# Attention and a gated layer on one core: GpSimd casts the higher part of a weight piece in the first four turns

## The chip, the cores and the metric

The kernel runs on one core of a Trainium2 chip. A core has five engines with an instruction queue each, which run in order and wait for one another by semaphores: TensorE (PE; its weight loads are listed as PEld), VectorE (DVE), ScalarE (ACT), GpSimd (POOL) and SyncE (SP), which issues most DMAs. The metric is the time of one execution on the device in microseconds (us), as a median of runs.

## The reference

Causal block attention for 8 batches of 8 heads, 576 tokens of 64 numbers each, then a gated layer on the 4608 tokens of 512 numbers:

```python
scores = scale * np.matmul(q, k.transpose(0, 1, 3, 2))
scores = np.where(block_i >= block_j, scores, -1000000000.0)   # blocks of 64 positions
attn = np.exp(scores - np.max(scores, axis=-1, keepdims=True))
attn = attn / (np.sum(attn, axis=-1, keepdims=True) + 1e-09)
x = np.matmul(attn, v)            # then [B, H, S, D] -> [B * S, H * D]
h = x @ w_in                      # w_in: 512 x 2048
out = (h * (1.0 / (1.0 + np.exp(-1.702 * h)))) @ w_out   # w_out: 2048 x 512
```

Everything comes in fp32. The weights w_in and w_out are stored as 64-bit numbers.

## The kernel before

**Turns.** Two heads make a pair, and there are 32 pairs. The main loop makes one turn per pair (turn 0 to turn 32). A turn does the scores of its pair (five row chunks 0 to 4, of widths 64, 192, 320, 448 and 576), the values (the product with v) of the pair before, and the transposition of q and k for the pair to come. The strings ORDER, START and HANDOVER give the order in a turn: digits are score chunks, L is `prep` (the two DVE transpositions of L297 that make `qk` for the next pair), V is `av`, and a, B, C are `flip` (PE transposes finished weights of attention, L102, and ACT copies them out of PSUM, L411 and L424; a takes chunks 0 and 1, B takes 2 and 3, C takes 4).

**One chunk** passes PE (scores, L99), DVE (a pass that masks, scales and finds the row's minimum, L351), ACT (exp with the row sum, L358), DVE (two tiny steps on the sums `sm`, L368 and L371), POOL (scaling by 1/sum, L376), then PE, ACT and PE again for B, C or a and V. V ends in two ACT copies into `xr` (L451, L450). DVE, ACT and POOL run in order, so an instruction that waits holds up all that stands behind it.

**Weight pieces.** There are 32 pieces of 128x512, in groups of four for w_in and four for w_out. A piece is converted in three steps. `begin` (L219): ACT takes the upper words into a PSUM bank of its own (tag w3, one buffer). `merge` (L223, L229, L234): DVE puts an fp32 number together in three instructions and writes it to a tile `wm` (two buffers in turn). `split_weights` (L243 and L82): a copy rounds that number to fp32r, the higher part (`wih` or `woh`), and POOL subtracts it to get the lower part (`wil` or `wol`). `begin` of the next piece follows `split_weights` in program order, and needs the bank that `merge` reads. `convert` spreads the pieces over turns by WEIGHTS_BY: by the end of turn 3 in program order 12 pieces are through, and by turn 8 all 32. On the engines they run later than in program order: the casts of those 12 pieces run from 20 us to 93 us. The tile scheduler puts each engine's instructions in an order by its own estimates of costs and by priorities, so PE's list and the lists of the other engines need not follow the text.

**The gated layer** (`moe`) is a generator from which `advance` takes work in step with the turns. It takes 384 tokens at a time (12 tiles, TILES). `split` makes a higher part `xh` (ACT, L498) and a lower part `xl` (DVE subtract, at L82) of the tokens. For each of 16 slices PE makes `hp` in 12 products (three for each of four parts of w_in), ACT and DVE make the gate `g` (L562, L563), ACT and POOL split it into `gh` and `gl` (L571, L82), and PE adds the slice to `acc`. `hp` has one PSUM bank, so the next slice waits until L563 has read the last one. The layer begins when the first batch's four pairs have their values, that is after V of turn 4.

The change touches `split_weights` alone; its line L243 is the cast on ACT, and the counter `turns["n"]` is the turn in program order (HP is 4).

Of the kernel before, what the change touches and what calls it, by code (L numbers as in the profile page):

```python
# [40 lines left out]
def attention_moe_kernel(  # L41
# [9 lines left out]
    nc = tc.nc  # L51
# [12 lines left out]
    HP = H // 2  # L64
# [6 lines left out]
    def f(ap):  # L71
        return ap.bitcast(F32)
# [8 lines left out]
    def subtract(eng, out, in0, in1):  # L81
        eng.tensor_tensor(out=out, in0=in0, in1=in1, op=ALU.subtract)  # L82
# [3 lines left out]
    turns = {"n": 0, "bank": 0, "experts": False}  # L86
# [37 lines left out]
    def weights(name, g):  # L124
        if (name, g) not in home:
            home[name, g] = room(f"{name}{g}", [P, 4, WC], F32R, name)
        return home[name, g]
# [111 lines left out]
    def split_weights(j):  # L239
        _, name, g, x = pieces[j]  # L240
        z = whole.pop(j)
        hi, lo = (weights(name + p, g)[:, x] for p in "hl")
        nc.scalar.copy(out=hi, in_=f(z))  # L243
        subtract(nc.gpsimd, lo, f(z), f(hi))

    def convert(upto):

        while conv["step"] < int(2 * upto):
            j, odd = divmod(conv["step"], 2)
            if odd:  # L250
                split_weights(j)
                if j + 1 < len(pieces):
                    load_weights(j + 3)
                    begin(j + 1)
            else:
                if j == 0:
                    begin(0)
                merge(j)
            conv["step"] += 1
# [405 lines left out]
```

## Time and profile before

| | us |
|---|---|
| median of 3 runs | 1117.67 (1117.2 to 1118.97) |
| span of the profiled execution, first to last instruction | 1116.9 |
| PE busy | 1082.2 (97% of the span) |
| DVE, ACT, POOL busy | 584.2, 498.9, 406.4 |
| PE busy from 200 us to the end | 909.5 of 917 |

The profiled execution is known by its span only, 1116.9 us; the median of the runs is 0.8 us longer, which lies around the span. PE is busy nearly all the time after the first fifth, so the table says little about what waits for what in the first 90 us, where the changed instructions run. For that stretch the trace is read in order of time, and the waits are read in windows.

### The profile page before, as it was taken

To read this page: it belongs to the slowest core of one execution; us is meant where nothing else is said; L and a number is where in the kernel's file an instruction comes from. 1 tells how busy PE (TensorE), PEld (TensorE's weight loads), DVE (VectorE), ACT (ScalarE), POOL (GpSimd) and SP (SyncE) were. 2 spreads that over 40 slices of the span, in tenths; PEclk is the share of its full clock that TensorE was granted. 3 is DMA by queue.
4 is the path that set the end of the run, shared out by engine and by line. 5 is a ranking of instruction groups with operands and counts; after the bars stand their busy time and mean duration, and the time that the engine had idled before them with its cause. 6 is when DMAs were issued, how large, how long until landed. Compare 5 with 4: busy or idle time off the path is not lost. (4 is left out here: it accounts for less than half of the span.)

```text
span 1116.9 us, 19972 instructions
## 1 busy us (share of the span) xinstructions
PE 1082.2 (97%) x6960; PEld 912.9 (82%) x6960; DVE 584.2 (52%) x1856; ACT 498.9 (45%) x1321; POOL 406.4 (36%) x509
## 2 busy tenths in 40 slices
PE   6979999999999999999999999999999999999998
PEld 4757777788888888888888888888888888899997
DVE  6786786655645645655555555645645654211210
ACT  5865775443533534534443443443444434322322
POOL 4665565332333333333333332333333333122222
PEclk8979999999999999999999999999999999999999
DMA  8634523342434433243443333344442332200000
GB/s 183 193 89 153 146 61 80 72 103 59 96 81 86 109 80 70 58 99 71 113 86 75 80 92 68 63 108 86 86 103 66 71 84 54 54 30 1 29 1 29
DMA packets 219365, 91.25 MB, mean 82 GB/s; under 512 B 197760, under 2 KB 197760, under 8 KB 219264
## 3 DMA queue, kind: packets, MB, share of 16 engines
q1 hardware_dynamic: 214528, 89.38, 34.1%
q8 instruction: 55, 0.90, 0.3%
q10 hardware_dynamic: 4736, 0.59, 0.3%
q14 instruction: 46, 0.38, 0.1%
HBM read 45.09 MB, written 9.44 MB: 49 GB/s over the span
## 5 line engine op out<-in xcount | busy, mean ns | idle before, releaser
L82 POOL TENSOR_TENSOR gl<-g,gh 128x384 fp32r<-128x384 f32 x192 | 194.5, 1013 | 555.1 <-ACT gh L571 450.4
L563 DVE SCALAR_TENSOR_TENSOR g<-g,hp 128x384 f32<-128x384 f32 x192 | 106.0, 552 | 318.6 <-ACT g L562 317.2
L99 PE MATMUL hp<-xh,wih 128*128 128x384 f32 x768 | 265.8, 346 | 2.8 <-DVE g L563 1.8
L562 ACT ACTIVATE g<-hp 128x384 f32<-128x384 f32 x192 | 94.2, 491 | 368.5 <-PE hp L99 361.0
L99 PE MATMUL hp<-xh,wil 128*128 128x384 f32 x768 | 258.7, 337 | 0.0
L99 PE MATMUL hp<-xl,wih 128*128 128x384 f32 x768 | 254.4, 338 | 0.2
L99 PE MATMUL acc<-woh,gh 128*128 128x512 f32 x576 | 233.9, 406 | 0.0
L99 PE MATMUL acc<-wol,gh 128*128 128x512 f32 x576 | 227.0, 394 | 0.0
L99 PEld LDWEIGHTS hp<-xh,wih 128*128 128x128 f32 x768 | 144.4, 188 | 30.9 <-DVE g L563 20.3
L99 PE MATMUL acc<-woh,gl 128*128 128x512 f32 x576 | 168.2, 393 | 0.3 <-POOL gl L82 0.3
L571 ACT CAST gh<-g 128x384 fp32r<-128x384 f32 x192 | 98.4, 513 | 156.8 <-DVE g L563 156.5
L99 PEld LDWEIGHTS hp<-xh,wil 128*128 128x128 f32 x768 | 144.6, 188 | 5.6
L358 ACT ACTIVATE e<-e,mx 64x64 f32<-64x64 f32 (+4 forms) x240 | 132.2, 552 | 32.2 <-DVE mx L351 32.2
L376 POOL TENSOR_TENSOR e<-e,sm 64x64 f32<-64x64 f32 (+1 forms) x192 | 113.6, 612 | 86.3 <-DVE sm L371 42.5
L99 PEld LDWEIGHTS hp<-xl,wih 128*128 128x128 f32 x768 | 144.0, 188 | 1.0 <-DVE xl L82 1.0
L99 PE MATMUL bank<-qk 64*128 64x320 f32 (+4 forms) x768 | 124.3, 432 | 16.2 <-DVE qk L297 10.4
L99 PEld LDWEIGHTS acc<-woh,gh 128*128 128x128 f32 x576 | 108.2, 188 | 34.2 <-issue 10.8
L99 PEld LDWEIGHTS acc<-woh,gl 128*128 128x128 f32 x576 | 107.6, 188 | 25.4 <-POOL gl L82 1.2
L351 DVE CUSTOM_DVE_ANT_0 e<-bank,mask 64x64 f32<-64x64 f32 (+4 forms) x240 | 89.7, 417 | 70.1 <-PE bank L99 67.0
L99 PEld LDWEIGHTS acc<-wol,gh 128*128 128x128 f32 x576 | 108.4, 188 | 16.8 <-issue 0.4
L385 DVE STREAM_TRANSPOSE turned<-e 128x384 f32<-128x384 f32 (+1 forms) x192 | 92.5, 500 | 49.5 <-POOL e L376 48.9
L99 PEld LDWEIGHTS bank<-qk 64*128 64x128 f32 x768 | 71.4, 196 | 56.4 <-issue 25.4
(50 smaller groups left out, 960.6 us busy)
## 6 DMA issues: line engine op xcount, KB each, us to landing
turned<-turned SPq DMA_DIRECT2D x192, 80.0 KB, 2.1
turned<-turned SPq DMA_DIRECT2D x96, 112.0 KB, 2.2
raw<-in_q_dram SPq DMA_DIRECT2D x128, 72.0 KB, 2.3
out_dram<-osb SPq DMA_DIRECT2D x36, 256.0 KB, 2.4
raw<-in_k_dram SPq DMA_DIRECT2D x120, 72.0 KB, 2.4
turned<-turned SPq DMA_DIRECT2D x96, 88.0 KB, 2.1
words<-in_moe_w_in_dram SPq DMA_DIRECT2D x16, 512.0 KB, 5.6
vp<-in_v_dram SPq DMA_DIRECT2D x60, 128.0 KB, 2.4
```

The source lines that it names most:

```text
L82: eng.tensor_tensor(out=out, in0=in0, in1=in1, op=ALU.subtract)
L99: return tc.keep_in_program_order(nc.tensor.matmul(**kw))
L351: nc.vector.tensor_tensor_reduce(out=e[0:m, hd, lo:hi], in0=s, in1=mk, op0=ALU.add, op1=ALU.min, scale=-0.125, scalar=3e38 if lo == 0 else ...
L358: nc.scalar.activation(out=e[0:m, hd], in_=e[0:m, hd], func=AF.Exp, scale=-1.0, bias=mx[0:m, i, hd : hd + 1], accum_out=sm[0:m, i, hd : hd ...
L376: nc.gpsimd.tensor_tensor(out=x, in0=x, in1=sc.to_broadcast([m, width(i)]), op=ALU.mult)
L385: nc.vector.transpose(out=tw[:, :, SLOT[i] : SLOT[i] + i, hd].rearrange("p b j c -> p j b c"), in_=e[:, hd, 0 : i * P],)
L562: nc.scalar.activation(out=g, in_=hp[:, 0:tt], func=AF.Tanh, scale=1.702)
L563: nc.vector.scalar_tensor_tensor(out=g, in0=g, scalar=1.0, in1=hp[:, 0:tt], op0=ALU.add, op1=ALU.mult)
L571: nc.scalar.copy(out=gh, in_=g)
```

## The change

In turns 0 to 3 (program order) the copy that makes the higher part of a weight piece is given to GpSimd. The subtraction behind it was on GpSimd already. 12 of the 32 casts move; from turn 4 on ACT casts as before.

```diff
         hi, lo = (weights(name + p, g)[:, x] for p in "hl")
-        nc.scalar.copy(out=hi, in_=f(z))
+        if turns["n"] < HP:
+            nc.gpsimd.tensor_copy(out=hi, in_=f(z))
+        else:
+            nc.scalar.copy(out=hi, in_=f(z))
         subtract(nc.gpsimd, lo, f(z), f(hi))
```

All later lines move down by three (L358 becomes L361, L376 becomes L379, and so on). PE's order and SP's order stay as they were, instruction by instruction. ACT, POOL and DVE get other orders. Three places follow; a name's number tells one buffer or piece from another.

ACT at the turn from pair 3 to pair 4, before (`wm_369`, `wm_430` and `wm_509` are the merged pieces 4, 5 and 6; `xr` takes the values of pair 2):

```order
L243 CAST woh_410<-wm_369 128x512
L219 ACTIVATE wm_416<-words_285 128x512
L243 CAST woh_410<-wm_430 128x512
L219 ACTIVATE wm_460<-words_414 128x512
L451 COPY xr_72<-bank_762 128x512
L450 COPY xr_72<-bank_763 128x64
L411 COPY turned_75<-bank_804 128x2x4x32
L498 CAST xh_977<-xr_72 128x384
L243 CAST woh_410<-wm_509 128x512
L219 ACTIVATE wm_519<-words_414 128x512
```

The same place now:

```order
L219 ACTIVATE wm_416<-words_285 128x512
L219 ACTIVATE wm_460<-words_414 128x512
L454 COPY xr_72<-bank_762 128x512
L453 COPY xr_72<-bank_763 128x64
L414 COPY turned_75<-bank_804 128x2x4x32
L501 CAST xh_977<-xr_72 128x384
L219 ACTIVATE wm_519<-words_414 128x512
```

The three casts are gone, and the `begin` of pieces 5, 6 and 7 (L219) stands directly behind what was in front of the casts.

POOL around the scaling of chunk 4 of pair 3, before (L376 is the scaling; `wm_369`, `wm_430` are pieces 4 and 5):

```order
L376 TENSOR_TENSOR turned_75<-turned_75,sm_620 128x448 x2
L376 TENSOR_TENSOR turned_75<-turned_75,sm_620 128x576 x2
L82 TENSOR_TENSOR wol_411<-wm_369,woh_410 128x512
L82 TENSOR_TENSOR wol_411<-wm_430,woh_410 128x512
L82 TENSOR_TENSOR wol_411<-wm_509,woh_410 128x512
```

POOL at the same place now (L244 is the cast, L379 the scaling):

```order
L244 CAST woh_410<-wm_369 128x512
L379 TENSOR_TENSOR turned_75<-turned_75,sm_620 128x576
L82 TENSOR_TENSOR wol_411<-wm_369,woh_410 128x512
L379 TENSOR_TENSOR turned_75<-turned_75,sm_620 128x576
L244 CAST woh_410<-wm_430 128x512
L82 TENSOR_TENSOR wol_411<-wm_430,woh_410 128x512
L244 CAST woh_410<-wm_509 128x512
L82 TENSOR_TENSOR wol_411<-wm_509,woh_410 128x512
```

A cast and a subtraction now stand between and in front of the two scalings, and each later subtraction has its cast right in front of it.

DVE where the gated layer begins, before (`wm_649` and `wm_674` belong to piece 9; `xl` is the lower part of the first 384 tokens, `g_1003` the first gate):

```order
L223 TENSOR_SCALAR wm_649<-wm_649 128x512
L229 SCALAR_TENSOR_TENSOR wm_649<-words_517,wm_649 128x512
L82 TENSOR_TENSOR xl_978<-xr_72,xh_977 128x384 x4
L234 SCALAR_TENSOR_TENSOR wm_674<-words_517,wm_649 128x512
L563 SCALAR_TENSOR_TENSOR g_1003<-g_1003,hp_990 128x384
```

DVE at the same place now:

```order
L223 TENSOR_SCALAR wm_649<-wm_649 128x512
L82 TENSOR_TENSOR xl_978<-xr_72,xh_977 128x384 x4
L229 SCALAR_TENSOR_TENSOR wm_649<-words_517,wm_649 128x512
L234 SCALAR_TENSOR_TENSOR wm_674<-words_517,wm_649 128x512
L566 SCALAR_TENSOR_TENSOR g_1003<-g_1003,hp_990 128x384
```

The four subtractions that make `xl` moved ahead of the second merge instruction of piece 9. Elsewhere on DVE the transpositions L297 of the turns 1 and 2 also changed places: in turn 2 the first of the two now stands three passes earlier than before, in turn 1 one pass and two small steps later.

## Rows read from the trace of the kernel before

**Rows 1.** The page: the span and the number of instructions.

```profile
span 1116.9 us, 19972 instructions
```

**Rows 2.** Windows: length, busy us by engine (instructions), granted clock, DMA share, GB/s.

```profile
20.00:40.00 20.00, 18.24 (x142) 13.76 (x141) 14.69 (x57) 15.41 (x50) 13.23 (x19) 0.84 0.68 153
...
60.00:80.00 20.00, 15.65 (x109) 11.67 (x109) 15.90 (x41) 14.76 (x42) 13.41 (x15) 0.66 0.51 125
...
84.00:200.00 116.00, 110.08 (x762) 88.54 (x761) 83.36 (x239) 77.80 (x206) 68.92 (x75) 0.99 0.40 107
200.00:1117.00 917.00, 909.51 (x5714) 778.20 (x5712) 439.39 (x1412) 362.79 (x944) 289.56 (x363) 1.00 0.32 72
```

**Rows 3.** Waits from 45 to 84 us: who waited for whom, total, times, longest.

```profile
PE bank L102 <- ACT xr L450: 2.1, 1, 2.1
...
ACT woh L243 <- DVE wm L234: 5.1, 3, 2.3
ACT wih L243 <- DVE wm L234: 3.0, 1, 3.0
...
DVE wm L223 <- ACT wm L219: 4.6, 5, 1.5
```

**Rows 4.** Groups by form up to 94 us (casts: 190 us): busy, mean ns, idle before.

```profile
L243 ACT CAST woh<-wm 128x512 fp32r<-128x512 f32 x16 | 9.9, 622 | 8.8 <-DVE wm L234 8.7
...
L82 POOL TENSOR_TENSOR wil<-wm,wih 128x512 fp32r<-128x512 f32 x8 | 10.2, 1275 | 8.2 <-ACT wih L243 8.2
...
L376 POOL TENSOR_TENSOR turned<-turned,sm 128x576 f32<-128x576 f32 x8 | 9.0, 1147 | 3.7 <-DVE sm L371 2.9 <-ACT xr L450 0.8
...
L156 POOL MEMSET turned<- 64x1024 f32 x1 | 0.9, 947 | 0.0
```

**Rows 5.** Turns 1 and 2 in time: start, length, instruction, idle before it.

```profile
20.50 2.25 POOL L376 TENSOR_TENSOR turned<-turned,sm 128x576 f32<-128x576 f32 x2 [1.65 <-DVE sm L371]
...
20.54 1.12 DVE L368 TENSOR_SCALAR sm<-sm 64x2 f32<-64x2 f32 x1
...
26.79 0.62 ACT L243 CAST wih<-wm 128x512 fp32r<-128x512 f32 x1 [1.62 <-DVE wm L234]
...
28.59 4.63 PE L99 MATMUL bank<-turned,vp 128*64 128x128 f32 x60 [1.58 <-ACT turned L411]
...
40.66 2.99 PE L99 MATMUL bank<-turned,vx 128*64 128x128 f32 x60
...
42.66 0.77 DVE L297 STREAM_TRANSPOSE qk<-raw 128x576 f32<-128x576 f32 x1
```

**Rows 6.** The L368 steps from 14 to 60 us: shortest/median/longest ns.

```profile
L368 DVE TENSOR_SCALAR sm<-sm x18: 152/194/1208, 14.5 to 58.2; 128x2 f32<-128x2 f32 x15, 64x2 f32<-64x2 f32 x3
```

**Rows 7.** Turn 3 into turn 4, in order of time.

```profile
60.51 1.33 PE L99 MATMUL bank<-qk 64*128 64x192 f32 x8 [2.52 <-DVE qk L297]
...
63.18 0.62 ACT L243 CAST woh<-wm 128x512 fp32r<-128x512 f32 x1 [2.29 <-DVE wm L234]
...
64.35 0.70 DVE L223 TENSOR_SCALAR wm<-wm 128x512 uint32<-128x512 uint32 x1 [1.21 <-ACT wm L219]
```

**Rows 8.** The start of the gated layer, in order of time.

```profile
77.66 3.50 DVE L82 TENSOR_TENSOR xl<-xr,xh 128x384 fp32r<-128x384 f32 x4
...
78.55 1.25 POOL L376 TENSOR_TENSOR turned<-turned,sm 128x448 f32<-128x448 f32 x1
...
81.78 0.62 ACT L243 CAST wih<-wm 128x512 fp32r<-128x512 f32 x1 [2.98 <-DVE wm L234]
...
83.44 0.44 PE L99 MATMUL hp<-xh,wih 128*128 128x384 f32 x1 [1.78 <-DVE g L563]
```

**Rows 9.** The tile `xl` on DVE, all 48: shortest/median/longest ns.

```profile
L82 DVE TENSOR_TENSOR xl<-xr,xh x48: 543/557/1353, 77.7 to 1042.1; 128x384 fp32r<-128x384 f32 x48
```

**Rows 10.** The third gate's lower part on POOL, and PE's use of it.

```profile
97.04 1.01 POOL L82 TENSOR_TENSOR gl<-g,gh 128x384 fp32r<-128x384 f32 x1 [2.94 <-ACT gh L571]
...
102.97 0.95 PE L99 MATMUL acc<-woh,gl 128*128 128x512 f32 x3
```

## The prediction, made before the changed kernel was run

> **What bounds the kernel now.** I read the span first, then windows, then the waits of the stretch in which the changed instructions run, then that stretch in order of time. From 200 us to the end PE is busy 909.51 of 917 us at a granted clock of 1.00, and from 84 to 200 us 110.08 of 116 [rows 2]. So once the gated layer has begun PE is the bound, with work that the change leaves alone, and whatever moves the point at which PE gets its second slice of that layer (83.44 us [rows 8]) moves the end by about as much. Before that point PE is not full: 15.65 of 20 us from 60 to 80, at a mean clock of 0.66 [rows 2]. There ACT, DVE and POOL are each busy 13 to 16 of 20 us, none of them full, and they wait for each other. The reader should see a ping-pong in the waits [rows 3]: ACT's cast waits for the merge on DVE (5.1 us for `woh`, 3.0 us for `wih`), DVE's next merge waits for ACT's `begin` (4.6 us), and PE waits 2.1 us for the copies L450 and L451, which stand on ACT behind the cast. ACT runs in order, so a cast that waits for a merge holds up copies and exps that were ready.
>
> **What the change removes and adds.** It removes 12 casts of 622 ns from ACT [rows 4], 7.5 us of busy time. That sum is worth nothing by itself; what counts is the casts that stand in the ping-pong. `begin` of the next piece still waits for the merge, since it writes the bank that the merge reads, so ACT still stops there; it only starts `begin` about 0.5 us sooner (an estimate: the cast's 0.62 less a tenth or so that neighbours on ACT overlap). It adds 12 casts to POOL, which no row shows. Below is a fill of 1024 elements in 947 ns, so 0.47 us for 512, which reads nothing. Above is the subtraction of the same shape, 1.275 us, which reads two tensors [rows 4]. Between lies the scaling, 576 elements in 1.147 us, so about 1.0 us for 512, with one tensor and one repeated number. I take 0.7 us, nearer to the fill, as the cast reads one operand; 12 of them are 8.4 us on POOL (5.6 to 15.3). POOL was busy 13 of 20 us, so it has room, but in order: what comes behind a cast waits for that piece's merge.
>
> **A mechanism that speaks against it.** The tiny step L368 takes 152 ns at its shortest and 1208 ns at its longest [rows 6]. The long one at 20.54 ran for 1.12 us, just while POOL's first scaling of chunk 4 ran, which began at 20.50 [rows 5]. The subtraction for `xl` takes 543 ns at its shortest and 1353 at its longest [rows 9], and the four of the first tile took 3.50 us at 77.66 while POOL was at work; a scaling of 448 elements at 78.55 took 1.25 us there [rows 8], longer than one of 576. So these DVE steps and POOL's work keep each other out. The Trainium skill says so too (SBUF — State Buffer, section Who interferes with whom): a VectorE instruction with two SBUF inputs, or in a two-port mode, and a GpSimd instruction that reads SBUF exclude each other, for a whole instruction, and the first to issue has it. By that rule more work on POOL holds up DVE, which the change is silent about, and the trace agrees (1208 against 152 ns). If nothing held DVE up, the sum below would be 3.6 us of gain and the time 1114.1; with it, it is 2.3 us.
>
> **The sum, by turn**, at the point where PE goes on.
>
> Turn 1, gain 1.3. The cast at 26.79 waited 1.62 us on ACT, and the copies for V stood behind it; V's products began at 28.59 after an idle 1.58 [rows 5]. Without the cast the copies come 0.7 us sooner; they are then limited by the exps, whose passes on DVE come some 0.5 us later in the new order. With a gap of about 0.7 us instead of 1.58 I expect V at the higher clock level: it took 4.63 us here and 2.99 one turn later [rows 5]. That alone would give 1.6 more, but turn 2's scores also need the transposition of q and k on DVE, which lets through about 0.6 of it. Ends: 0.7 (V stays slow) to 1.4. Against this, POOL now does a cast and a subtraction ahead of the second scaling of chunk 4, which ends near 24.7 instead of 22.75 (20.50 + 2.25 [rows 5], plus 0.7 and 1.275). What hides it: PE's transposes of that chunk feed ACT copies that cannot run before about 27, because of the exps. Without that cover it would cost up to 1.2.
>
> Turn 2, loss 0.8. No piece is converted here. But the first transposition (0.77 us [rows 5]) now stands ahead of three passes, on the way to the last exps, the last L368 and the second transposition, for which turn 3's scores wait. Ends: 0 to 0.8.
>
> Turn 3, gain 0.3. DVE is nearly full, with three merges. Its longest wait for `begin`, 1.5 us [rows 3], stood ahead of the first passes of the turn; in the new order two passes of width 64 and one of 192 go first, which fills about 0.6 us of it. Two L368 steps come right behind a merge, just when POOL starts a cast, and I charge 0.3 for both. Ends: a gain of 0.8, a loss of 0.4.
>
> Turn 4, gain 1.5. From its first scores (60.51, after an idle 2.52 for the transposition [rows 7]) pieces 5 and 6 are merged back to back before any pass. The cast at 63.18 came between merge 5 and `begin` of piece 6, and DVE waited 1.21 us until 64.35 [rows 7]. Taking out the casts of pieces 4, 5 and 6 gives 0.5 each, so 1.5 for the exps of the turn, and 1.0 of it for the copies that PE waits for. Then the new order hands most of it back: merge 8 now runs ahead of a pass of chunk 3, and the lead is down to 0.3 at the last exp of that chunk. From there to the gate three things go: a copy L411 that now comes earlier (0.5), cast 8 (0.5), and the rest of merge 9, which now runs behind `xl`, beside PE's products with it, together with cast 9, which stood at 81.78 in front of the gate, 1.2 in all. That is 2.5. Against it stands the exclusion: before, one `xl` subtraction waited (1353 less 543, 0.8 us). Now POOL's cast 8 pushes its scalings of chunks 2 and 3 into the whole stretch, and each `xl` can meet one; I charge two more waits, 1.0 in all after what overlaps. Ends: 0 to 2.2.
>
> After the gate the third `gl` moves behind the two scalings of chunk 4 and a cast, 2.3 + 0.7 = 3.0 us later. It was ready at 98.05 and first used at 102.97 [rows 10], so 4.9 us of slack hide it; without that PE would wait for it in full.
>
> Together 1.3 - 0.8 + 0.3 + 1.5 = 2.3 us. The profiled span of 1116.9 us [rows 1] becomes 1114.6; the runs' median lies 0.8 above that span, so **1115.4 us**.
>
> **The rivals.** *The clock comes back.* PE ran at a mean 0.66 from 60 to 80 us. If fewer gaps keep it at the higher level, its 15.65 us of work shrink by a third, 5.3 us, and perhaps half of that lies on the way to the gate: 2.6 us more, 1112.8. For it: PE's 2.1 us of waiting for L450 shrink [rows 3]. Against it: the 2.52 us of idle time ahead of 60.51 stay, and ACT's exps still limit the copies.
>
> *The lead is handed back.* All four `xl` subtractions wait for a scaling each (about 0.95, so 3.8 less the 0.8 of now, so 3.0 against the 2.5 of turn 4), and turn 3 gives nothing, DVE being full: 1.3 - 0.8 + 0 - 0.5 leaves nothing, 1117.7. For it: the order of POOL there; against it: the scalings may be through earlier.
>
> *Slower: POOL keeps DVE out.* In 6 of the 12 pieces the new order has an L368 right behind the last merge instruction, or one tiny step later, and the end of the merge is what starts the cast. If the cast wins each time and costs as much as a subtraction, that is 6 x 1.275 = 7.7 us on DVE, plus 1.0 at `xl`, less the gross gain of 3.6: 5.1 us slower, 1122.8. The point from which it decides: 0.43 us for each of the six makes the change worth nothing, 0.8 us makes it slower by over 0.2%. For it: DVE is nearly full in turns 3 and 4. Against it: where L368 comes directly behind the merge it is already queued when the cast is still waiting for a semaphore, and a cast of 0.7 us is too short.
>
> **How the numbers follow.** The forecast, 1114.0 to 1116.6 with 1115.4 likeliest, has 0.52; the clock's return 0.20; the lead handed back 0.16; the slower case 0.12. About 0.2%, 2.2 us, is what a measurement of this kernel can tell from no change, and the forecast sits on that bound: a little over half of it (0.28) counts as faster, the rest (0.24) as the same. Faster is 0.28 + 0.20 = 0.48, same 0.24 + 0.16 = 0.40, slower 0.12. The range goes down to the clock case, 1112.8, and up to 1119.2, which takes in a cast as long as a subtraction with half of the slower case's holds; beyond both I leave out about 0.17.
>
> **What would show it.** In the profile of the changed kernel: 12 casts on POOL at 0.5 to 1.0 us, none on ACT before about 93 us; V of turn 1 near 27.9 and at 3 us; turn 3's scores within 0.5 us of where they were; the first scores of turn 4 some 0.8 us sooner; the ACT waits for L234 still there, but in front of L219; the second slice of the gated layer near 81.1; PE's idle time behind it as before. I am wrong if the casts take over 1.2 us, if L368 grows to a median over 0.5 us up to 94 us, if the second slice starts after 83.4, or if PE's idle time from there to 200 us grows by over 1 us.

## The result, and the profile after

The changed kernel takes **1121.39 us** (median of 8 runs, 1119.8 to 1125.8) against 1117.65 us (8 runs, 1117.18 to 1119.27) for the kernel before on the same chip: ratio 1.0035, 95% interval 1.0023 to 1.0047. It is slower by 3.7 us. The forecast was 1115.4, its range ended at 1119.2, and slower had a chance of 0.12.

One number ahead of the prediction has to be put right. The kernels' runs are listed with both time and span, and 1.7 to 2.2 us lie between the two (1119.8 and 1117.7 in the profiled run of the changed kernel). So the profiled execution of before, with its span of 1116.9 [rows 1], must be the run of 1118.97 us, 1.3 above the median, and not a run whose median "lies 0.8 above". The forecast subtracted its gain from the median, so this didn't move it. It matters for the two traces, though: the profiled run of before is 1.3 us over its median, that of the change 1.6 us under its own, and their spans differ by 0.8 us where the medians differ by 3.7.

The changed kernel's page, and its windows beside [rows 2] (length, busy us by engine with instructions, granted clock, DMA share, GB/s):

```profile
span 1117.7 us, 19976 instructions
```

```profile
20.00:40.00 20.00, 17.52 (x151) 12.63 (x151) 15.16 (x63) 16.06 (x51) 15.59 (x22) 0.96 0.71 164
60.00:80.00 20.00, 15.82 (x112) 11.72 (x112) 16.53 (x43) 12.25 (x37) 15.39 (x19) 0.74 0.49 125
84.00:200.00 116.00, 107.82 (x749) 85.83 (x748) 83.04 (x236) 75.85 (x204) 68.71 (x76) 0.99 0.40 107
200.00:1117.00 917.00, 910.85 (x5715) 779.52 (x5713) 439.83 (x1412) 362.83 (x944) 289.61 (x363) 1.00 0.31 72
```

Up to 80 us the clock is higher than before (0.96 and 0.74 against 0.84 and 0.66). The loss is in the third row: from 84 to 200 us PE is busy 107.82 us where it was 110.08.

PE in order of time in the changed kernel, to be laid beside [rows 5, 7, 8] (start, length, instruction, idle time before it and what ended it):

```profile
27.99 2.98 PE L99 MATMUL bank<-turned,vp 128*64 128x128 f32 x60 [0.46 <-ACT turned L414]
...
32.56 0.76 PE L99 MATMUL bank<-qk 64*128 64x192 f32 x8 [0.78 <-DVE qk L300]
...
59.84 0.76 PE L99 MATMUL bank<-qk 64*128 64x192 f32 x8 [2.34 <-DVE qk L300]
...
81.05 0.44 PE L99 MATMUL hp<-xh,wih 128*128 128x384 f32 x1 [1.42 <-DVE g L566]
```

V of turn 1 starts 0.60 us sooner and lasts 2.98 instead of 4.63 us; turn 4's first scores come 0.67 us sooner; the second slice of the gated layer comes at 81.05 instead of 83.44. So a lead of 2.4 us is there, as forecast, on one execution of each. It is gone 60 us later. One mark per turn shows where: the start of V's sixty products. V of turn 5, 6 and 7, first in the kernel before, then in the changed kernel:

```profile
114.02 2.98 PE L99 MATMUL bank<-turned,vp 128*64 128x128 f32 x60
...
141.57 2.98 PE L99 MATMUL bank<-turned,vp 128*64 128x128 f32 x60
...
169.37 2.99 PE L99 MATMUL bank<-turned,vp 128*64 128x128 f32 x60
```

```profile
110.20 2.99 PE L99 MATMUL bank<-turned,vp 128*64 128x128 f32 x60
...
141.52 2.99 PE L99 MATMUL bank<-turned,vp 128*64 128x128 f32 x60
...
169.44 2.99 PE L99 MATMUL bank<-turned,vp 128*64 128x128 f32 x60
```

At V of turn 5 the lead reads 3.8 us, more than the second slice gave. In the profiled run of before the granted clock fell behind PE's wait of 1.78 us at 83.44 [rows 8]. In before_nowait, a kernel of the experiments that differs from before in the weights of one later slice alone, the same wait of 1.78 us left it at 1.00. From 84 to 88 us, first before, then before_nowait:

```profile
84.00:88.00 4.00, 4.00 (x15) 3.76 (x14) 2.38 (x5) 0.90 (x3) 1.02 (x1) 0.57 0.00 0
```

```profile
84.00:88.00 4.00, 4.00 (x21) 2.93 (x19) 2.73 (x5) 1.97 (x4) 2.06 (x3) 1.00 0.00 0
```

That is 4 x 0.43 = 1.7 us which before's trace lost there by bad luck. before_nowait and before_extra, in which before's order is kept too, start V of turn 5 at 111.58 and 112.10, so the lead there is 1.4 to 1.9 us.

From V of turn 5 to V of turn 6 is 27.55 us before and **31.32 us** after: 3.8 us lost in turn 6. From turn 6 to 7 it is 27.80 and 27.92. Inside turn 6 PE waits, in the changed kernel, in slice 8 of the first tile:

```profile
133.78 0.45 PE L99 MATMUL hp<-xh,wih 128*128 128x384 f32 x1 [0.45 <-ACT wih L246]
...
136.20 0.44 PE L99 MATMUL hp<-xh,wil 128*128 128x384 f32 x1 [1.98 <-POOL wil L82]
```

Slice 8 is the first that needs the third group of w_in, and its fourth part is piece 19. POOL in order of time around it, first before, then after (L376 and L379 are the scaling of turn 6's chunk 2; the `wil` rows are the subtractions of pieces 18 and 19):

```profile
132.70 1.27 POOL L82 TENSOR_TENSOR wil<-wm,wih 128x512 fp32r<-128x512 f32 x1
134.22 1.02 POOL L82 TENSOR_TENSOR gl<-g,gh 128x384 fp32r<-128x384 f32 x1 [0.25 <-ACT gh L571]
135.20 1.28 POOL L82 TENSOR_TENSOR wil<-wm,wih 128x512 fp32r<-128x512 f32 x1
137.89 1.40 POOL L376 TENSOR_TENSOR turned<-turned,sm 128x320 f32<-128x320 f32 x2 [1.41 <-DVE sm L371]
```

```profile
130.05 1.29 POOL L82 TENSOR_TENSOR wil<-wm,wih 128x512 fp32r<-128x512 f32 x1
131.29 1.02 POOL L82 TENSOR_TENSOR gl<-g,gh 128x384 fp32r<-128x384 f32 x1
133.52 1.40 POOL L379 TENSOR_TENSOR turned<-turned,sm 128x320 f32<-128x320 f32 x2 [1.21 <-DVE sm L374]
134.88 1.27 POOL L82 TENSOR_TENSOR wil<-wm,wih 128x512 fp32r<-128x512 f32 x1
```

Before, piece 19 stands ahead of the scaling; after, behind it. The scaling waits 1.21 us for DVE, piece 19 waits with it, and PE, which came 4.6 us sooner to slice 8 (131.52 against 136.09), finds the piece only 0.32 us sooner (134.88 against 135.20).

POOL's order is the smaller part of it, though: the subtraction starts 1.15 us behind the end of ACT's cast of the piece (133.73) where it was 0.35, so 0.8 us later. The larger part lies ahead of POOL. ACT's cast of piece 19 and PE's first product of slice 8, in the kernel before, in the change, and in only4, a kernel of the experiments in which the order is before's:

```profile
134.23 0.62 ACT L243 CAST wih<-wm 128x512 fp32r<-128x512 f32 x1
136.09 0.42 PE L99 MATMUL hp<-xh,wih 128*128 128x384 f32 x1
```

```profile
131.52 0.42 PE L99 MATMUL hp<-xh,wih 128*128 128x384 f32 x1
133.11 0.62 ACT L246 CAST wih<-wm 128x512 fp32r<-128x512 f32 x1
```

```profile
130.53 0.63 ACT L246 CAST wih<-wm 128x512 fp32r<-128x512 f32 x1
132.37 0.42 PE L99 MATMUL hp<-xh,wih 128*128 128x384 f32 x1
```

The cast starts 1.86 us ahead of PE's slice before, and 1.59 us behind it in the change. It is not the lead that does this: only4 is at V of turn 5 as early as the change (110.32 against 110.20), and there the cast is 1.84 us ahead. The lists of DVE and ACT differ. In the change DVE's two passes of chunk 2 stand ahead of the last merge step of piece 19, and ACT's exps of that chunk ahead of its cast; before, the merge step and the cast came first.

Nothing near this place was edited: casts of piece 12 and later are on ACT in both kernels. What changed is the order that the scheduler gave the later instructions; that the edit changed its estimates is the likely reason, which no run shows. And the wait is not all of it. The same windows, before and then after:

```profile
136.00:140.00 4.00, 4.00 (x23) 3.02 (x21) 3.05 (x8) 3.32 (x9) 2.59 (x4) 1.00 0.76 242
140.00:144.00 4.00, 4.00 (x58) 3.45 (x58) 3.06 (x10) 2.95 (x7) 2.06 (x3) 1.00 0.79 130
```

```profile
136.00:140.00 4.00, 3.80 (x12) 2.42 (x12) 2.56 (x7) 2.38 (x5) 1.53 (x3) 0.71 0.41 158
140.00:144.00 4.00, 4.00 (x56) 3.45 (x56) 2.52 (x7) 2.30 (x6) 2.72 (x4) 0.86 0.53 88
```

Behind the wait the granted clock is 0.71 and 0.86 of the 2.4 GHz level where it was 1.00, a stretch at 1.2 GHz. That is 4 x 0.29 + 4 x 0.14 = 1.7 us of lost work. The waits of 0.45 and 1.98 and this make 4.1; against it a wait earlier in the turn is shorter (1.21 us for ACT's copies before, 0.42 for DVE after). That leaves 3.3 of the 3.8 us explained.

### The profile page after: what moved, and what is told of

Same layout as the page of the kernel before. It is cut to its first block, busy times and chain, and to the rows that moved or that the text cites. A ratio compares the mean times of both kernels' runs of the same rounds, so it can differ in the third digit from the quotient of the medians.

```text
span 1117.7 us, 19976 instructions
## 1 busy us (share of the span) xinstructions
PE 1079.8 (97%) x6960; PEld 911.6 (82%) x6960; DVE 586.0 (52%) x1856; ACT 492.7 (44%) x1309; POOL 413.6 (37%) x521
## 5 line engine op out<-in xcount | busy, mean ns | idle before, releaser
L361 ACT ACTIVATE e<-e,mx 64x64 f32<-64x64 f32 (+4 forms) x240 | 132.2, 552 | 32.2 <-DVE mx L354 32.2
L379 POOL TENSOR_TENSOR e<-e,sm 64x64 f32<-64x64 f32 (+1 forms) x192 | 113.6, 612 | 86.4 <-ACT e L361 42.4
L99 PE MATMUL bank<-qk 64*128 64x320 f32 (+4 forms) x768 | 121.8, 427 | 17.1 <-DVE qk L300 11.4
```

The costliest lines, as they stand in the source:

```text
L99: return tc.keep_in_program_order(nc.tensor.matmul(**kw))
L361: nc.scalar.activation(out=e[0:m, hd], in_=e[0:m, hd], func=AF.Exp, scale=-1.0, bias=mx[0:m, i, hd : hd + 1], accum_out=sm[0:m, i, hd : hd ...
L379: nc.gpsimd.tensor_tensor(out=x, in0=x, in1=sc.to_broadcast([m, width(i)]), op=ALU.mult)
```

## The experiments

Fifteen kernels, each compared with the kernel before on its own chip (medians there 1117.9 to 1118.2). Three theories came up, in this order. *Lead turned into idle time* (supply theory in the first expectations): PE comes sooner, the weights do not, so the lead becomes a wait and the wait lowers the clock. *GpSimd keeps DVE out* (exclusion theory there): casts on POOL hold DVE's steps. *Order*: what costs is not the casts, but the order that the scheduler gives turns 5 to 8 because of them. The ratio weighs all runs and is not the quotient of the two medians. "V 5 to 7" is the time from V of turn 5 to V of turn 7 in the profiled run, so in one execution, which can be the fastest (the change, next8, mid4, before_fill) or the slowest (first6, nine) of its kernel's; the last column says how the subtractions of pieces 13 to 31 stand among POOL's other rows in the built program.

| kernel | us | ratio to before (95%) | V 5 to 7 | order of pieces 13 to 31 |
|---|---|---|---|---|
| before | 1117.65 | | 55.35 | before's |
| before_nowait | 1117.72 | 0.9996 (0.9986 to 1.0005) | 55.33 | before's |
| before_extra | 1117.49 | 0.9999 (0.9990 to 1.0008) | 55.33 | before's |
| only4 | 1116.89 | 0.9993 (0.9983 to 1.0003) | 55.24 | before's |
| first4 | 1116.35 | 0.9988 (0.9976 to 0.9999) | 55.24 | before's |
| first5 | 1117.38 | 0.9994 (0.9985 to 1.0004) | 55.26 | before's |
| first6 | 1117.41 | 0.9994 (0.9985 to 1.0003) | 55.25 | before's |
| nine | 1118.39 | 1.0005 (0.9996 to 1.0014) | 54.61 | 13, 21, 23 and 24 one row earlier |
| the change | 1121.39 | 1.0035 (1.0023 to 1.0047) | 59.24 | 13, 17, 19 to 21 later (four rows, one, two, one, one); 23, 24 earlier |
| next8 | 1119.24 | 1.0020 (1.0006 to 1.0034) | 59.22 | as the change |
| mid4 | 1120.74 | 1.0027 (1.0015 to 1.0038) | 59.88 | as the change, 14 later too |
| only6 | 1122.22 | 1.0042 (1.0029 to 1.0055) | 58.46 | 13, 17, 21 later (four rows, two, one); 23 to 25 earlier |
| only8 | 1121.50 | 1.0034 (1.0021 to 1.0047) | 58.48 | as only6, 14 later too |
| after_nowait | 1122.87 | 1.0026 (1.0009 to 1.0043) | 57.37 | as the change |
| after_fill | 1118.77 | 1.0014 (1.0001 to 1.0027) | 58.06 | as the change, but 20 as before |
| to20 | 1125.09 | 1.0055 (1.0035 to 1.0074) | 60.03 | 13 three rows later; 18, 21, 23 to 25, 27, 30 earlier |
| before_fill | 1121.20 | 1.0026 (1.0011 to 1.0040) | 56.66 | none later; 21, 23 to 25, 27, 30 earlier, up to five rows |

**Is it the wait at slice 8?** Two kernels take it away: slice 8 of the first tile multiplies its fourth part with weights of an earlier group, in the changed kernel and in the kernel before.

```diff
-  lhsT=weights(wa, fc // FG)[:, dc, fs]
+  lhsT=weights(wa, fc // FG - (t == 0 and fc == 8 and dc == 3))[:, dc, fs]
```

after_nowait:

> The changed kernel, in which slice 8 of the first 384 tokens takes its weights for the fourth part of w_in (pieces 11 and not 19) from the group before, so that it waits for nothing of piece 19; the amount of work is the same and that one slice computes with other weights. Supply theory (the lead of 2.4 us at the gate, 4.5 us by slice 8, is lost because PE comes to slice 8 before piece 19 is split): PE's 2.0 us wait for the lower part at 136 us goes, the clock stays at its higher level from 136 to 144 us, 3 to 4 us are saved against the changed kernel (1121.4), so 1116.5 to 1118.5 in runs, with a span near 1114. Exclusion theory (GpSimd's casts hold VectorE up everywhere): nothing changes, 1120.5 to 1122.

before_nowait:

> The kernel before, with the same other weights for slice 8 of the first 384 tokens. Supply theory: piece 19 comes just in time there, so at most 0.5 us is saved, 1117.2 to 1117.7. Exclusion theory: no change either, 1117.7.

The wait at slice 8 was gone in after_nowait and V of turn 6 came 26.7 us behind V of turn 5, quicker than before. The time did not follow: the median was 1122.87 us, where the supply theory had 1116.5 to 1118.5, and the ratio of 1.0026 can't be told from the change's 1.0035. PE now waited behind V of turn 6 (PE in order of time):

```profile
142.06 0.63 PE L102 MATMUL bank<-ident,turned 128*64 128x128 f32 x4 [0.75 <-ACT xr L454]
145.12 1.38 PE L99 MATMUL bank<-qk 64*128 64x256 f32 x6 [0.52 <-ACT xr L453]
148.04 0.80 PE L99 MATMUL bank<-qk 64*128 64x320 f32 x2 [1.54 <-DVE mx L354]
```

So one wait removed was another one made, one turn on. These waits are those of a run of 1118.47 us, the second fastest of ten; what the median lost beyond that is not in this trace. The kernel before doesn't care (1117.72): it never waited there. This spoke for something wider than piece 19.

**Is it idle time that lowers the clock?** Nine products more ahead of slice 8, which the real ones overwrite, give PE 1.6 us of work where it would wait.

```diff
+  if t == 0 and fc == 8:
+      for wa, xb, dc in terms[:9]:
+          mm(out=hp[:, 0:tt], lhsT=weights(wa, fc // FG)[:, dc, fs], rhs=xb[:, dc, 0:tt], ...)
```

after_fill, in the changed kernel:

> The changed kernel with 9 more products (1.6 us of PE work) ahead of slice 8 of the first 384 tokens, a repetition of its first three parts that is thrown away. Supply theory with the clock as its second half: the products lie inside the wait of 2.4 us, PE is idle under 1 us, the clock stays at its higher level from 136 to 144 us, and the time falls by 1 to 1.7 us against the changed kernel, to about 1120. If the wait alone cost the time and the clock nothing: no change, 1121.4. If neither matters: longer by 1.6, 1123.

before_fill, in the kernel before:

> The kernel before with the nine added, thrown-away products ahead of slice 8 of the first tile, 1.6 us of TensorE's work at full clock, as they stood in the changed kernel's filled version, which measured 2.6 us under the changed kernel. Theory 'idle time that lowers the granted clock': before has no wait at slice 8, so here the same products cost what they last or less, where a later wait takes some of it: 1118 to 1119.4 us, 0.3 to 1.7 above before. If the products bring time back here too (1116 or less), then what they do has nothing to do with the wait that the change made.

after_fill took 1118.77 us, 2.6 under the changed kernel with more work in it (2.3 by the ratios, whose intervals still overlap). The wait shrank:

```profile
135.75 0.44 PE L99 MATMUL hp<-xh,wil 128*128 128x384 f32 x1 [1.15 <-POOL wil L82]
```

and the clock stood at 1.00 from 132 us on, which fits that the wait's price was in good part the clock behind it. before_fill was to show that the same products only cost in the kernel without the wait, 0.3 to 1.7 us; it cost 3.3 (1121.2), with single runs from 1117.95 to 1125.34. The added products had given it another order behind slice 8 as well (V 5 to 7 is 56.66 us, 1.3 over before's, in the fastest of its ten runs). As a control it is inconclusive.

**Do the casts keep DVE out?** before_extra has ACT's casts and the same twelve casts on POOL besides, written where the subtraction writes later. Nothing is relieved, POOL is as busy as in the changed kernel.

```diff
         nc.scalar.copy(out=hi, in_=f(z))
+        if turns["n"] < HP:
+            nc.gpsimd.tensor_copy(out=lo, in_=f(z))
```

> The kernel before, with ACT's casts as they are, and twelve casts of the same size more on GpSimd, which write a copy into the lower half's tile that the subtraction then overwrites: GpSimd is as busy as in the changed kernel, ACT is not relieved, no lead is made. Theory 'lead turned into idle time': GpSimd's added 12 x 0.6 us lie in its own idle time, 1117 to 1119 us; a little of it may show where a piece's subtraction is late by 0.6 us. Theory 'GpSimd keeps DVE out': the whole loss without the gain, 1121 to 1124 us.

It took 1117.49 us, no difference. The added casts and the tiny step on `sm` (the L368 of [rows 6]) in it, the first with count, busy and mean ns, the second with shortest, median and longest ns up to 60 us:

```profile
L245 POOL CAST wil<-wm 128x512 fp32r<-128x512 f32 x8 | 4.9, 612 | 8.5 <-DVE wm L234 6.0 <-DVE sm L373 2.4
```

```profile
L370 DVE TENSOR_SCALAR sm<-sm x18: 154/248/1204, 14.6 to 57.6; 128x2 f32<-128x2 f32 x15, 64x2 f32<-64x2 f32 x3
```

The casts run at 612 ns and the median step rises from 194 to 248 ns; the end does not move. This theory fell.

**Which of the twelve?** first4 moves the casts of pieces 0 to 3 alone, next8 those of pieces 4 to 11.

```diff
-        if turns["n"] < HP:
+        if j < 4:              # first4
+        if 4 <= j < 12:        # next8
```

> Only pieces 0 to 3 are cast on GpSimd (they are split before the first turn); pieces 4 to 11 go back to ACT. Theory 'lead turned into idle time': little of the lead is made (the twelve casts give 2.4 us by the second slice of the gated layer, most of it in turns 1 to 4), the second slice comes 0 to 0.8 us ahead of the kernel before, so nothing is lost behind it: 1116.9 to 1118.5 us, within 0.2% of before. Theory 'GpSimd keeps DVE out' (each POOL cast makes DVE's work beside it late): a third of the loss of 3.7 us, 1118.5 to 1119.5 us. If instead the loss sits in the start (note loads, first casts), this kernel keeps all of it: about 1121.

> Only pieces 4 to 11, those split inside the first four turns, are cast on GpSimd. Theory 'lead turned into idle time': the lead at the second slice is made by these eight, so it is 1.5 to 2.4 us there, PE waits again for the lower half of piece 19 at slice 8 of the first tile, and the time is that of the change, 1120 to 1121.5 us. Theory 'GpSimd keeps DVE out': two thirds of the loss, about 1120. Theory 'the loss sits in the start': 1117.7, as before.

first4 took 1116.35 us, ahead of before; next8 1119.24, behind it, with the wait at slice 8 (1.98 us at 134.60) as in the change. By the lead theory this was plausible, since the eight make the lead. But laid side by side the built programs told something else: first4 has the order of before on ACT, DVE and POOL in every row behind the first slice's gate, and next8 has on POOL that of the change. The lead and the order had changed together in every slower variant of the change so far, to20 among them, which moves the casts of pieces 0 to 19:

> The changed kernel with the casts of pieces 0 to 19 on GpSimd and not 0 to 11. Supply theory: pieces 12 to 19 lose the cast between merge and begin as well, piece 19 is split 2 us sooner or more, the wait at slice 8 falls under 0.5 us, and the time is 1114 to 1117. Exclusion theory: eight more casts on GpSimd hold VectorE up more, slower than the changed kernel by 1 to 3 us, 1122 to 1124.

It took 1125.09 us. Its wait at slice 8 was gone too, and it waited behind V of turn 6 and in turn 8 instead (1.62 us for ACT's `xr` copy at 144.95, 1.83 for POOL's scaling at 188.46). More weights sooner, and slower: the lead theory had expected a gain. The other theory had the size, but before_extra had taken its reason away.

**Order or lead?** Subsets of casts were chosen by the order that their programs have. first6 (pieces 0 to 5) has before's order in every row behind the first slice's gate, as first4 has; nine (0 to 5 and 9 to 11) has another on ACT and DVE, but its pieces come at before's places or a row earlier; mid4 (4 to 7) has the change's; only6 moves one cast, and yet gets a later order.

```diff
-        if turns["n"] < HP:
+        if j in (0, 1, 2, 3, 4, 5):               # first6
+        if j in (0, 1, 2, 3, 4, 5, 9, 10, 11):    # nine
+        if j in (6,):                             # only6
+        if j in (4, 5, 6, 7):                     # mid4
```

> Pieces 0 to 5 cast on GpSimd. In this program the subtractions of pieces 13 to 31 stand between the same scalings and GELU steps of GpSimd as in the kernel before; in the changed kernel piece 13 stands four of those rows later, piece 17 one, piece 19 two, piece 20 one, piece 21 one. Theory 'order': what costs is that later order, which the six casts do not bring, so the lead of 0.7 to 1.5 us is kept: 1115.5 to 1117 us, and no wait of TensorE for the lower half at slice 8. Theory 'lead turned into idle time': half the casts, half the loss: 1118.5 to 1120 us.

> Pieces 0 to 5 and 9 to 11 cast on GpSimd, nine of the change's twelve. In this program piece 13 stands one row of GpSimd's earlier than in the kernel before, piece 21 one earlier and piece 23 one earlier, and 14 to 20 stand as before. Theory 'order': the lead of 1.5 to 2.4 us at the second slice of the gated layer is kept, no wait at slice 8 over 0.5 us: 1114.5 to 1117 us. Theory 'lead turned into idle time': PE is as far ahead as in the changed kernel and the pieces come no sooner, so the wait of 1 to 2 us at slice 8 and the clock's fall stay: 1120 to 1121.5 us.

> One cast alone on GpSimd, that of piece 6. It relieves ACT by 0.62 us, but with it the later order is like the changed kernel's: piece 13 stands four rows of GpSimd's later than in the kernel before, piece 17 two later, pieces 21 and 23 one later, piece 25 two earlier; piece 19 stands as before. Theory 'order': 1118.5 to 1121 us with a lead of 0.5 us at the most, the subtraction of piece 13 1 to 2 us late against the scores around it. Theory 'lead turned into idle time' and theory 'GpSimd keeps DVE out': one cast of twelve, 1117 to 1118.2 us, no change.

> Pieces 4 to 7 cast on GpSimd: as many casts as in the kernel with pieces 0 to 3, which measured 1116.35 us. Here the later order is the changed kernel's: piece 13 four rows of GpSimd's later than before, piece 17 one, piece 19 two, 20 and 21 one. Theory 'order': slower than before, 1119 to 1121 us, with a wait of TensorE at slice 8 for the lower half of piece 19. Theory 'lead turned into idle time': a third of the lead, a third of the loss, 1118 to 1119 us; the wait at slice 8 is under 1 us.

first6 took 1117.41, nine 1118.39, mid4 1120.74 and only6 **1122.22 us**. Six and nine casts cost nothing that can be measured; one cast costs 4.3 us. The lead theory had given only6 no change and nine the full loss, and was wrong on both. The order theory was too hopeful, though: first6 came 0.4 and nine 1.4 us above its ranges, which had the lead kept in full, and only6 came 1.2 us above its range. (The expectations of only6 and only8 put piece 23 a row later; it stands a row earlier.) In only6 PE loses its time at another place than in the change, at turn 7's third chunk of scores; first PE there, then the window behind it, then DVE:

```profile
150.39 0.80 PE L99 MATMUL bank<-qk 64*128 64x320 f32 x2 [1.66 <-DVE mx L354]
```

```profile
150.00:154.00 4.00, 3.61 (x11) 2.86 (x11) 3.50 (x11) 2.27 (x6) 2.24 (x2) 0.68 0.53 180
154.00:158.00 4.00, 4.00 (x28) 3.37 (x27) 2.62 (x12) 2.88 (x10) 1.28 (x1) 0.90 0.00 0
```

```profile
148.84 0.69 DVE L234 SCALAR_TENSOR_TENSOR wm<-words,wm 128x512 uint32<-128x512 uint32 x1 [0.46 <-DVE wm L229]
149.44 0.55 DVE L566 SCALAR_TENSOR_TENSOR g<-g,hp 128x384 f32<-128x384 f32 x1
149.91 0.42 DVE L354 CUSTOM_DVE_ANT_0 turned<-bank,mask 128x256 f32<-128x256 f32 x1
```

In the kernel before the gate `g` runs ahead of that last merge instruction, DVE has no 0.46 us wait there, and PE waits 0.34 us instead of 1.66. The other 0.85 us of the difference come from ahead of it: this merge starts 6.71 us behind V of turn 6 in only6 and 5.86 before, and in the merge two pieces earlier a transposition now stands ahead of the last step (L300 at 140.94, 0.77 us). The 1.3 us more, and 4 x 0.32 + 4 x 0.10 = 1.7 us of lower clock behind them, are the 2.5 us by which turn 6 to 7 is longer in only6 (30.30 against 27.80), with half a microsecond to spare.

**Is it piece 6 itself?** only4 and only8 move one cast each: piece 4 with before's order in all rows but one, piece 8 with only6's kind of order. first5 (pieces 0 to 4) is one more kernel in before's order.

```diff
-        if turns["n"] < HP:
+        if j in (4,):                # only4
+        if j in (8,):                # only8
+        if j in (0, 1, 2, 3, 4):     # first5
```

> One cast alone on GpSimd, that of piece 4. The rows of ACT and DVE stand in this program exactly as in the kernel before (ACT's one cast taken out), GpSimd's too but for one. Theory 'order': no change, 1117.0 to 1118.3 us. Theory 'a single cast on GpSimd is dear in itself' (it holds DVE, or its piece is late): as the kernel with the cast of piece 6, 1120 to 1122.5 us.

> One cast alone on GpSimd, that of piece 8, which stands some 15 us behind piece 6. The later order changes as in the kernel with the cast of piece 6: piece 13 four rows of GpSimd's later than before, piece 17 two, piece 21 and 23 one, piece 25 two earlier; piece 8 itself two earlier and piece 14 two later. Theory 'order': slower again, 1119.5 to 1122.5 us, with a wait of TensorE for DVE's mx at turn 7 of over 1 us as in that kernel. Theory 'it was piece 6 in its own place': no change, 1117 to 1118.3 us.

> Pieces 0 to 4 cast on GpSimd; the later order is before's, as with pieces 0 to 3 (1116.35 us, 1.5 under before) and 0 to 5 (1117.41 us, 0.5 under). Theory 'order, and the lead is kept': 1116 to 1117.2 us. Theory 'order, and the lead is worth nothing behind the gate': 1117.4 to 1118.2 us, as before.

only4 took 1116.89 us, only8 1121.50, and first5 1117.38 (ratio 0.9994), on the bound between its two expectations and not to be told from the kernel before. So a cast on POOL is not dear in itself and piece 6 is nothing special. only8 waits where only6 does, by the same amount:

```profile
149.22 0.80 PE L99 MATMUL bank<-qk 64*128 64x320 f32 x2 [1.67 <-DVE mx L354]
```

V of turn 5, 6 and 7 in only4 and then in only6:

```profile
110.32 2.99 PE L99 MATMUL bank<-turned,vp 128*64 128x128 f32 x60
...
137.82 2.98 PE L99 MATMUL bank<-turned,vp 128*64 128x128 f32 x60
...
165.56 2.98 PE L99 MATMUL bank<-turned,vp 128*64 128x128 f32 x60
```

```profile
112.08 2.99 PE L99 MATMUL bank<-turned,vp 128*64 128x128 f32 x60
...
140.24 2.98 PE L99 MATMUL bank<-turned,vp 128*64 128x128 f32 x60
...
170.54 2.98 PE L99 MATMUL bank<-turned,vp 128*64 128x128 f32 x60
```

Over all kernels the time from V of turn 5 to V of turn 7 splits in two: 54.6 to 55.4 us where pieces 13 to 31 stand on POOL at before's places or a row earlier, with medians of 1116.35 to 1118.39; 56.7 us and more in all the others, with medians of 1118.77 to 1125.09. A piece that stands later is not the common cause, since in before_fill none does and in to20 one alone; POOL's list marks another order, and the loss lies where that order makes PE wait. Nor does the time of this stretch give the median: next8 and the change have the same 59.2 us and medians of 1119.24 and 1121.39.

What stays open: no kernel was run with all twelve casts moved and the order of before. So order and lead are told apart by kernels with fewer casts, not in the change itself. The nearest are only4 and first5: they start V of turn 5 at 110.32 and 110.41, as early as the change (110.20), keep before's order, and lose nothing in turn 6. Why moving piece 6 or piece 8 changes its order, and piece 4 does not, was not looked into. And why the lead of six or nine casts at the second slice doesn't show in the median is not settled: the profiled runs of first6 and nine have a clock of 0.94 and 0.92 from 84 to 100 us and reach V of turn 5 at 111.78 and 112.51, later than only4 with its one cast (110.32). Later, from V of turn 8 to V of turn 9, the profiled runs take 28.8 to 33.2 us, whatever their order (28.91 in before, 30.43 in before_nowait, 31.64 in first6). In all of them PE waits there 2.5 to 3.0 us for DVE, and the clock behind that wait differs. So a lead of 2 us is hard to follow beyond that point.

## Why the prediction was wrong, point by point

**The casts.** Right. Twelve of them stand on POOL (mean ns behind the busy sum), near the 0.7 us that was taken from between a fill and a scaling:

```profile
L244 POOL CAST wih<-wm 128x512 fp32r<-128x512 f32 x8 | 4.9, 610 | 9.1 <-DVE wm L234 6.3 <-DVE sm L371 2.7
...
L244 POOL CAST woh<-wm 128x512 fp32r<-128x512 f32 x4 | 2.4, 608 | 1.4 <-DVE sm L371 1.2 <-DVE wm L234 0.2
```

**The sum by turn.** Right to some tenths, on one profiled execution of each: turn 2's scores 1.40 us sooner (1.3 was forecast for turn 1), turn 3's 0.68 (0.5 by then), turn 4's 0.67 (0.8), the second slice 2.39 (2.3). Agreement to a tenth is partly luck: before_nowait, the same program as before up to there, has its second slice at 82.56 and not 83.44. V of turn 1 was forecast near 27.9 and 3 us and came at 27.99 with 2.98.

**The mechanism that speaks against it.** It is there, and no run shows that it costs time at the end. In the changed kernel the step L371 (before, L368) took, up to 60 us as in [rows 6] (shortest, median, longest ns):

```profile
L371 DVE TENSOR_SCALAR sm<-sm x18: 141/170/1605, 14.6 to 58.3; 128x2 f32<-128x2 f32 x15, 64x2 f32<-64x2 f32 x3
```

The longest step grew from 1208 to 1605 ns, the median fell from 194 to 170; up to 94 us, the stretch of the forecast's sign, it is 170 in both kernels. The four `xl` of the first tile took 3.83 us instead of 3.50, and PE waited 0.73 us for them at 78.72. The Trainium skill (SBUF — State Buffer, section Who interferes with whom) has VectorE and GpSimd shut each other out for whole instructions under its conditions; single steps of over 1.2 us agree with that, and before_extra, with twelve more casts and no change of time, in which PE waits for `xl` as well (0.62 us), shows that it is not what decides here. The rival "POOL keeps DVE out" had the right sign and about the right size (1122.8), for a reason that the runs refute.

**The step that failed** is the first paragraph of the prediction: once the gated layer has begun, PE is the bound "with work that the change leaves alone", and what moves the second slice "moves the end by about as much"; its last part has it again as "PE's idle time behind it as before". That idle time went from 5.92 to 8.18 us between 84 and 200 us, 2.3 more, which the prediction had named as the sign that it is wrong. PE's instructions were the same in the same order, but PE is not fed by itself there. Until about 190 us pieces 13 to 31 are still converted on ACT, DVE and POOL, beside the scores of turns 5 to 8 and the gated layer. The order of these was changed and the prediction did not ask what the new one does; it followed the changed order only up to the third `gl`, which PE uses at 102.97 [rows 10], though the whole order could be read beforehand. The term that is missing in the sum is turn 6: +3.8 us. Against the 2.3 us of gain it makes the change 1.5 us slower; against the 1.4 to 1.9 us by which it leads before_nowait and before_extra at V of turn 5, 1.9 to 2.4 us. Its trace stands at 2.0 to 2.5 us behind these two at V of turn 7 (169.44 against 166.91 and 167.43) and still so at the end (spans of 1117.7 against 1115.3 and 1115.5). The rest of the 3.7 us is not in that execution: it is the fastest of the eight, and the others, at a mean clock of 0.985 to 0.989 over the span (0.989 in it), take 1120.25 to 1125.8. What they lost beyond it stays open.

**The third `gl`.** It was forecast 3.0 us later at no cost. It came sooner: at 92.46, so 11.4 us behind the second slice where it was 13.6 (97.04 [rows 10]), though the two scalings of chunk 4 now stand ahead of it. PE does not wait for it in either kernel.

**The clock.** "The clock comes back" was right up to 80 us (0.74 against 0.66). That the clock can be lost again behind a wait made later stood in no rival.

## What to carry to other kernels

Where a scheduler sets the order by its estimates, an edit of one engine's work at the start can change the program far behind it. Lay the built programs side by side up to the last place where the touched engines still feed the bound one, and look for steps that now stand behind a row that waits. Test with an edit that has the same instructions and keeps the order, or a tiny one that changes it: here one cast of 0.61 us, moved, made 4.3 us, and six moved casts made none. Take a profiled run for one execution: before's own trace held 1.7 us of lower clock that before_nowait's and before_extra's did not have. Of this change, the version to keep is the part that leaves the order alone: the casts of pieces 0 to 3, 1116.35 us, a gain of 0.12% whose interval (0.9976 to 0.9999) only just leaves out no change, and which the two neighbours in the same order, first5 and first6, bear out only in sign (0.9994 both).

## What the runs showed of the hardware

A GpSimd cast from fp32 to fp32r of 128x512 took 0.61 us, less than half of the subtraction of that shape (1.27 us) and about what ACT takes (0.62 us [rows 4]).

A wait of PE of 1.7 to 2.0 us in a stretch that was otherwise busy was followed by a granted clock of 0.68 to 0.71 over the next 4 us in the changed kernel and in only6. Each time this lost about 1.7 us, nearly as much as the wait itself. It is not a fixed price: with work put into the wait and 1.15 us of it left (after_fill) the clock stayed at 1.00, and so it did behind the three waits of after_nowait that are shown above, 2.8 us in all. Even the same wait went both ways: 1.78 us ahead of the second slice was followed by 0.57 in before and by 1.00 in before_nowait and before_extra, and 2.6 us at 205 us was followed, from 206 to 210, by 1.00 in before and 0.58 in the change. So what a wait costs in clock can't be read from one execution.
